# A state-space layer and its feed-forward block on one core: the first product of the later groups as seven block products, in a new order

## The chip, the core and the metric

The kernel runs on one core of a Trainium2 chip. The core has TensorE (PE; its weight loads are listed apart as PEld), VectorE (DVE), ScalarE (ACT), GpSimd (POOL) and SyncE (SP), which here issues the DMAs. Each engine works off its own queue. The metric is the time of one execution in device microseconds, lower is better. All arithmetic is fp32.

## The reference

The first part is a Mamba-2 scan over 4 batches, 8 heads, 768 positions, head size 32 and state size 16; the second is a feed-forward block over the 3072 tokens with 256 features:

```
y = ssd(x, a, B, C)              # intra-chunk products, plus state carried between chunks
x = y transposed to (3072, 256)
h = x @ w_in                     # 256 -> 2048
g = h * sigmoid(1.702 * h)
out = g @ w_out                  # 2048 -> 256
```

The weights and the scan inputs are drawn at random; `w_in` and `w_out` reach the kernel as 64-bit floats and are rounded to fp32 on VectorE and ScalarE in the first group.

## The kernel before

The tokens are cut into six groups g = 0 to 5 of 512. A group is made of four chunks of 128 tokens, and two chunks are a pair p, so that group g consists of pairs 2g and 2g + 1. Everything is transposed for the products: `yT[g]` holds the scan's result, features by tokens, in two 128-row halves.

The scan. `load(p)` (L102) fetches B, C and x of a pair, six DMAs; `spread` (L198) fetches a chunk's decays from a scratch tensor, repeated over 128 partitions. `decay` (L313) runs one VectorE scan of 1024 elements for each chunk, and `ends` (L359) multiplies B by its last column. `turn` (L422) transposes B and C on TensorE (tp), copies them on ScalarE and scales them on VectorE (CsT). `gain` and `keep` (L490, L503) form a pair's share of the state (A, S). `score` (L457) multiplies C and B (cb, 32-row tiles, into a PSUM area of four banks) and `weigh` (L473) multiplies the result by the decays in one VectorE instruction of 2048 elements a pair. `finish` (L522) adds the inter-chunk part (L536) and the intra-chunk part (L547) in two PSUM banks and copies them to `yT` on ScalarE.

The first product. `hidden(g, f)` (L563) multiplies one of 16 blocks of 128 columns of `w_in` by `yT[g]`: two matmuls of 512 columns into one PSUM bank, and a Silu on ScalarE into half of `gT[g, j]`, with j = f // 2. So `gT[g, j]` is 256 hidden features by 512 tokens.

The second product. For group 0 it is plain (`project_all`, L582). From group 1 on it goes by Strassen's method in Winograd's form: `gT[g, j]` and the 256 x 256 block of `w_out` are taken as 2 x 2 blocks, `mix_w` (L602) forms four sums of weight blocks once, and `mix_g` (L617) four sums of activation blocks on VectorE, three instructions for each j. `product(g, j)` (L625) issues seven matmuls of 256 columns, each adding to its own accumulator in the four-bank area over the eight j. At the end of a group, `combine` (L658) copies two accumulators out on ScalarE and does five additions on VectorE; `give` (L676) transposes the result back and stores it. The last group ends in `end` (L685), which takes the products of j = 5 to 7 one accumulator after another.

The order is written by hand. Steps H0 to H7 (two `hidden`) and P0 to P7 (one `product`) alternate, with the H steps three ahead (five in group 1), and the table `after[g]` hangs the rest on steps. `in_order` (L20) ties each engine's instructions to the order in which the program issues them. So an instruction that waits on TensorE, VectorE or ScalarE holds all that were issued after it on that engine.

The program takes eight banks of PSUM: four in the area (cb, ab, acc) and four (`bank`, L421) that are handed out in turn to everything else. The pools in SBUF that matter are `raw` (four buffers each for B, C, x), `gT` (eight buffers, shared by `gT`, the mixed blocks, u and c of `combine`), and the wide buffers of the weight rounding ("m", "p2").

Of the kernel before, what the change touches and what calls it, by code (L numbers as in the profile page):

```python
# [8 lines left out]
FP32 = mybir.dt.float32  # L9
U32 = mybir.dt.uint32  # L10
AF = mybir.ActivationFunctionType
ALU = mybir.AluOpType
# [22 lines left out]
def kernel(  # L35
# [27 lines left out]

    nc = tc.nc
# [27 lines left out]
    ps = ctx.enter_context(tc.tile_pool(name="ps", bufs=4, space=bass.MemoryType.PSUM))  # L92
    dram = ctx.enter_context(tc.tile_pool(name="dram", bufs=1, space=bass.MemoryType.DRAM))


    az = const.tile([P, NC, P], FP32, name="az")
    az0 = const.tile([P, CG, P], FP32, name="az0")
# [4 lines left out]
    def load(p):  # L102
        rb[p] = raw.tile([P, 2, NH, N], FP32, tag="b", name=f"b{p}", bufs=4)
        rc[p] = raw.tile([P, 2, NH, N], FP32, tag="c", name=f"c{p}", bufs=4)
        rx[p] = raw.tile([P, 2, NH, D], FP32, tag="x", name=f"x{p}", bufs=4)
        for dst, src in ((rb, B), (rc, C), (rx, x)):
            for k in range(2):
                b, c = divmod(2 * p + k, NC)
                sl = slice(c * P, (c + 1) * P)
                nc.sync.dma_start(out=dst[p][:, k], in_=src[b, :, sl, :].rearrange("h s d -> s h d"))  # L110
# [100 lines left out]
    def spread_rows(b):  # L211
        raf[b] = raw.tile([P, NC, P], FP32, tag="af", name=f"af{b}", bufs=2)
        nc.sync.dma_start(out=raf[b].rearrange("p c s -> p (c s)"),
                          in_=a[b].unsqueeze(1).to_broadcast([NH, N, S]))
# [22 lines left out]
    for p in range(PG, 2 * PG):  # L237
        load(p)
# [52 lines left out]
    same = const.tile([P, NH, D], FP32, name="same")  # L291
# [132 lines left out]
    def area(name):  # L424
        return ps.tile([P, R, 4 * P], FP32, tag="cb", name=name, bufs=1)

    def turn_only(p):
# [13 lines left out]
        if p < PG:  # L441

            s["tp"] = ssd.tile([P, 2, P], FP32, tag="CsT", name=f"C{p}", bufs=4)
            nc.scalar.activation(s["tp"], tp[:, 1], AF.Copy)

    def since_start(p):
# [5 lines left out]
        s["CsT"] = ssd.tile([P, 2, P], FP32, tag="CsT", name=f"CsT{p}", bufs=4)  # L452
# [69 lines left out]
    def finish(p, late=False):  # L522
        g, half = divmod(p, PG)
        b, c = divmod(2 * p, NC)
        s = st.pop(p)
        L = Ls.pop(p)
        if half == 0:
            yT[g] = ffn.tile([P, NK, TG], FP32, tag="yT", name=f"yT{g}")
        y = [bank(f"y{p}_{t}")[:, :2 * P].rearrange("p (k i) -> p k i", k=2)
             for t in range(NK)]  # L530

        def inter(k, start, stop):
            old = state[p][:, 0] if k else state[p - 1][:, 1]
            for t in range(NK):
                rows = slice(HB * N * t, HB * N * (t + 1))
                nc.tensor.matmul(  # L536
                    out=y[t][:, k], lhsT=old[rows], rhs=s["CsT"][rows, k],
# [3 lines left out]
        inter(0 if c else 1, True, False)  # L541
        if c and not late:
            inter(1, False, False)
        for k in range(2):
# [6 lines left out]
        if c and late:  # L551
            inter(1, False, True)
        state.pop(p - 1, None)
        for t in range(NK):
            nc.scalar.activation(  # L555
                yT[g][:, t, 2 * half * P:2 * (half + 1) * P],
                y[t].rearrange("p k i -> p (k i)"), AF.Copy)
# [4 lines left out]

    def hidden(g, f):  # L563
        j, i = divmod(f, 2)
        if i == 0:
            gT[g, j] = ffn.tile([P, 2, TG], FP32, tag="gT", name=f"gT{g}_{j}", bufs=NF // 2)
# [5 lines left out]
        nc.scalar.activation(gT[g, j][:, i], h, AF.Silu, scale=GELU_SCALE)  # L572

# [43 lines left out]
    def mix_g(g, j):  # L617

        B = gT[g, j].rearrange("p i (t e) -> p i t e", t=2)
        t = mixed_g[g, j] = ffn.tile([P, 4, HT], FP32, tag="gT", name=f"mg{g}_{j}", bufs=NF // 2)  # L620
        nc.vector.tensor_tensor(out=t[:, 0:2], in0=B[:, :, 1], in1=B[:, 0], op=ALU.subtract)  # L621
        nc.vector.tensor_tensor(out=t[:, 2], in0=B[:, 1, 1], in1=t[:, 0], op=ALU.subtract)  # L622
        nc.vector.tensor_tensor(out=t[:, 3], in0=B[:, 1, 0], in1=t[:, 2], op=ALU.subtract)  # L623

    def product(g, j, only=range(7)):  # L625
        if j == 0:
            a = area(f"acc{g}").rearrange("p r (t e) -> p (r t) e", t=2)
            acc[g] = [a[:, i] for i in range(7)], a
            if g == NG - 1:

                for i in range(4, 7, 2):
                    b = bank(f"acc{g}_{i}").rearrange("p (t e) -> p t e", t=2)
                    acc[g][0][i:i + 2] = [b[:, 0], b[:, 1]]
# [7 lines left out]
        for i in only:  # L641
            lhsT, rhs = terms[i]
            nc.tensor.matmul(out=acc[g][0][i], lhsT=lhsT, rhs=rhs,  # L643
                             start=(j == 0 and i % 2 == 0), stop=(j == NF // 2 - 1),
                             skip_group_check=True)

    def copies(g):
        u = ffn.tile([P, 4, HT], FP32, tag="gT", name=f"u{g}", bufs=NF // 2)
        c = ffn.tile([P, 2, 2, HT], FP32, tag="gT", name=f"c{g}", bufs=NF // 2)
        done[g] = u, c  # L650

        nc.scalar.activation(u[:, 0:4:3], acc[g][1][:, 0:4:3], AF.Copy)  # L652
        return u, c
# [31 lines left out]
    def end(g, j0):  # L685
# [27 lines left out]
        for i in (1, 0):  # L713
            cols = slice(i * P, (i + 1) * P)
            turn_out(g, 1, (i,), o[1 + i])
            ob = ffn.tile([P, 2, TG], FP32, tag="gT", name=f"ob{g}_1_{i}", bufs=NF // 2)
# [57 lines left out]
    narrow(1)  # L774

# [31 lines left out]
    at(in_project[0], 14, lambda: finish(PG + 1))  # L807
    for k in range(PG):
        at(in_project[0], 5 + 3 * k, lambda k=k: load(2 * PG + k))
# [3 lines left out]
    after = [{} for _ in range(NG)]  # L813
    for g in range(1, NG):
        n, places = (g + 1) * PG, after[g]
        chunks = range((g + 2) * CG, (g + 3) * CG) if g + 2 < NG else ()
        if g == 1:
            def late(p):
                gain(p)
                keep(p)  # L820
                score(p)
                weigh(p)

            at(places, "H0", lambda: decay(2 * CG), lambda: decay(2 * CG + 1), lambda: turn(n1))
            n1 = n
            at(places, "H1", lambda: late(n1), lambda: decay(2 * CG + 2),
               lambda: decay(2 * CG + 3), lambda: turn(n1 + 1))
            at(places, "H3", lambda: finish(n1), lambda: late(n1 + 1))
            at(places, "H4", lambda: finish(n1 + 1))
            for k, i in enumerate(("H4", "P0", "P2", "P4")):  # L830
                at(places, i, lambda k=k: mix_w(k))
            for j in range(NF // 2):
                at(places, f"P{j - 1}" if j else "H4", lambda j=j: mix_g(1, j))
        else:
            at(places, "H1", lambda g=g: mix_g(g, 0), lambda g=g: give(g - 1))
            if g + 1 < NG:
                at(places, "H0", lambda n=n: gain(n + 1), lambda n=n: keep(n + 1),
                   lambda n=n: score(n), lambda n=n: weigh(n))
                at(places, "H1", lambda n=n: score(n + 1), lambda n=n: weigh(n + 1))
            at(places, "H2", lambda g=g: mix_g(g, 1))  # L840
            for j in range(2, NF // 2):
                at(places, f"P{j - 2}", lambda g=g, j=j: mix_g(g, j))
            if g + 1 < NG:
                at(places, "H2", lambda n=n: finish(n))
                at(places, "P0", lambda n=n: finish(n + 1))
        for k, c in enumerate(chunks):
            at(places, f"P{k + 1}", lambda c=c: decay(c))
        if g + 2 < NG:
            for k in range(PG):
                p = (g + 2) * PG + k  # L850
                at(places, f"P{5 + k}", lambda p=p: turn(p))
                if k == 0:
                    at(places, "P5", lambda p=p: gain(p), lambda p=p: keep(p))
# [7 lines left out]
    for g in range(1, NG):  # L861
        if g + 2 < NG:
            for k in range(PG):
                load((g + 2) * PG + k)
            for b in range(NB):
                if (g + 2) * CG <= b * NC < (g + 3) * CG:
                    spread_rows(b)
                    at(after[g], "P4", lambda b=b: clip_rows(b), lambda b=b: decay_rows(b))
        ahead = 5 if g == 1 else 3
        steps = [f"H{j}" for j in range(ahead)]  # L870
        for j in range(NF // 2):
            steps += [f"P{j}"] + ([f"H{j + ahead}"] if j + ahead < NF // 2 else [])
        for step in steps:
            j = int(step[1:])
            if step[0] == "H":
                hidden(g, 2 * j)
                hidden(g, 2 * j + 1)
            elif g < NG - 1 or j < 5:
                product(g, j)
            for do in after[g].get(step, []):  # L880
                do()
            if g + 2 < NG and step in ("H1", "H3"):
                for k in range(2):
                    spread((g + 2) * CG + k + (2 if step == "H3" else 0))
        if g < NG - 1:
            combine(g)
# [33 lines left out]
```

## Time and profile before

| | us |
|---|---|
| median of three runs | 393.74 (393.49 to 393.83) |
| the profiled execution, its own time | 397.72 |
| its span | 396.0 |

The profile is of that one execution. Its parts count in different ways: busy time is what an engine spent in instructions, and weight loads (PEld) lie beside matmuls. The chain that ended last is followed back from the last instruction, at each step to what released it. Line numbers are those of the kernel before.

Busy time in stretches of the span, in us:

| stretch | TensorE | VectorE | ScalarE |
|---|---|---|---|
| 0 to 20 | 17.01 | 13.15 | 6.02 |
| 20 to 60 | 38.06 | 35.56 | 22.08 |
| 60 to 100 | 40.00 | 31.63 | 11.36 |
| 100 to 140 | 40.00 | 32.18 | 11.50 |
| 140 to 180 | 40.00 | 27.08 | 9.89 |
| 180 to 220 | 40.00 | 21.31 | 8.79 |
| 220 to 260 | 40.00 | 23.46 | 9.46 |
| 260 to 300 | 39.98 | 20.28 | 10.63 |
| 300 to 340 | 40.00 | 8.48 | 7.02 |
| 340 to 380 | 40.00 | 12.49 | 9.34 |
| 380 to 396 | 11.96 | 4.75 | 2.66 |

The largest groups on TensorE are the first product's entries (L569, 384 of them, 173.3 us) and the second's (L643, 560 in four groups by their operands). A matmul's recorded length overlaps that of the next one. The weight loads of the second product take 190 ns each.

### The profile page before, as it was taken

To read this page: it belongs to the slowest core of one execution; us is meant where nothing else is said; L and a number is where in the kernel's file an instruction comes from. 1 tells how busy PE (TensorE), PEld (TensorE's weight loads), DVE (VectorE), ACT (ScalarE), POOL (GpSimd) and SP (SyncE) were. 2 spreads that over 40 slices of the span, in tenths; PEclk is the share of its full clock that TensorE was granted. 3 is DMA by queue.
4 is the path that set the end of the run, shared out by engine and by line. 5 is a ranking of instruction groups with operands and counts; after the bars stand their busy time and mean duration, and the time that the engine had idled before them with its cause. 6 is when DMAs were issued, how large, how long until landed. Compare 5 with 4: busy or idle time off the path is not lost.

```text
span 396.0 us, 5009 instructions
## 1 busy us (share of the span) xinstructions
PE 387.0 (98%) x2024; PEld 246.9 (62%) x2024; DVE 230.4 (58%) x348; ACT 108.7 (27%) x201; POOL 10.2 (3%) x32
## 2 busy tenths in 40 slices
PE   7989999999999999999999999999999999999995
PEld 2543447787556778566668566667566567556674
DVE  3959999993879696754574753572661131423133
ACT  3226857210432112322112231213231211321210
POOL 5000000010000001000000000000000000000000
PEclk9599999999999999999999999999999999999999
DMA  8989566920988000097000080000010000010001
GB/s 144 241 240 155 188 213 151 171 106 8 150 262 119 21 1 2 0 276 96 2 0 0 2 263 3 0 0 2 2 55 2 0 0 0 2 53 0 0 2 53
DMA packets 85790, 29.52 MB, mean 75 GB/s; under 512 B 75720, under 2 KB 79240, under 8 KB 85768
## 3 DMA queue, kind: packets, MB, share of 16 engines
q1 hardware_dynamic: 85672, 29.07, 31.1%
q8 instruction: 16, 0.26, 0.3%
q10 hardware_dynamic: 96, 0.13, 0.1%
q14 instruction: 6, 0.05, 0.0%
HBM read 25.95 MB, written 3.24 MB: 74 GB/s over the span
## 4 chain that ended last, share of the span: by engine, by line
PE 95%; DVE 3%; issue 1%; POOL 0%
PE h L569 41%; PE acc L643 31%; PE o L588 7%; PE cb L468 3%; PE busy L345 3%; PE y L547 3%; PE y L536 2%; PE tp L432 1%; PE ab L327 1%; PE oT L673 1%; PE A L496 1%; PE rows L403 1%; DVE L L479 1%; DVE L L354 1%; DVE w_in L181 0%
## 5 line engine op out<-in xcount | busy, mean ns | idle before, releaser
L569 PE MATMUL h<-yT,w_in 128*128 128x512 f32 x384 | 173.3, 596 | 0.8 <-DVE w_in L181 0.8
L569 PEld LDWEIGHTS h<-yT,w_in 128*128 128x128 f32 x384 | 71.5, 190 | 79.5 <-issue 73.0
L572 ACT ACTIVATE gT<-h 128x512 f32<-128x512 f32 x96 | 57.2, 596 | 172.8 <-PE h L569 134.5
L621 DVE TENSOR_TENSOR mg<-gT 128x512 f32<-128x512 f32 x40 | 27.5, 688 | 94.8 <-ACT gT L572 91.7
L643 PE MATMUL acc<-mg,mw 128*128 128x256 f32 x240 | 58.0, 379 | 0.0
L643 PEld LDWEIGHTS acc<-mg,mw 128*128 128x128 f32 x240 | 45.6, 190 | 6.2
L643 PE MATMUL acc<-gT,w_out 128*128 128x256 f32 x160 | 41.7, 384 | 0.0
L319 DVE TENSOR_TENSOR_SCAN L<-a,idents 128x1024 f32<-128x1024 f32 x18 | 41.1, 2282 | 0.0
L643 PEld LDWEIGHTS acc<-gT,w_out 128*128 128x128 f32 x160 | 29.5, 190 | 15.0 <-issue 11.5
L479 DVE TENSOR_TENSOR L<-L,cb 128x2048 f32<-128x2048 f32 (+1 forms) x13 | 27.5, 2122 | 6.8 <-PE cb L468 6.4
L588 PE MATMUL o<-w_out,gT 128*128 128x256 f32 x128 | 29.3, 383 | 0.0
L588 PEld LDWEIGHTS o<-w_out,gT 128*128 128x128 f32 x128 | 23.8, 190 | 4.1 <-issue 0.7
L643 PE MATMUL acc<-gT,mw 128*128 128x256 f32 x80 | 23.5, 379 | 0.0
L643 PE MATMUL acc<-mg,w_out 128*128 128x256 f32 x80 | 23.5, 379 | 0.0
L555 ACT ACTIVATE yT<-y 128x256 f32<-128x256 f32 x24 | 7.9, 381 | 44.0 <-PE y L547 40.8
L623 DVE TENSOR_TENSOR mg<-gT,mg 128x256 f32<-128x256 f32 x40 | 17.0, 425 | 1.4
L622 DVE TENSOR_TENSOR mg<-gT,mg 128x256 f32<-128x256 f32 x40 | 17.0, 425 | 1.4
L354 DVE TENSOR_TENSOR_SCAN L<-ab,idents 128x512 f32<-128x512 f32 x12 | 13.8, 1204 | 5.9 <-PE ab L327 5.9
L643 PEld LDWEIGHTS acc<-mg,w_out 128*128 128x128 f32 x80 | 15.2, 190 | 2.1
L643 PEld LDWEIGHTS acc<-gT,mw 128*128 128x128 f32 x80 | 15.2, 190 | 2.1
L656 DVE TENSOR_TENSOR u<-acc,u 128x256 f32<-128x256 f32 (+1 forms) x10 | 5.3, 531 | 17.5 <-ACT u L652 14.3
L468 PE MATMUL cb<-CT,BT 32*128 32x256 f32 x192 | 14.9, 422 | 0.2
(86 smaller groups left out, 258.4 us busy)
## 6 DMA issues: line engine op xcount, KB each, us to landing
a<-scratch SPq DMA_DIRECT2D x18, 512.0 KB, 5.4
bits<-in_moe_w_out_dram SPq DMA_DIRECT2D x4, 1024.0 KB, 5.4
x<-in_x_dram SPq DMA_DIRECT2D x24, 128.0 KB, 4.1
out_dram<-ob SPq DMA_DIRECT2D x11, 256.0 KB, 2.2
bits<-in_moe_w_in_dram SPq DMA_DIRECT2D x4, 512.0 KB
bits<-in_moe_w_in_dram SPq DMA_DIRECT2D x2, 1024.0 KB
b<-in_B_dram SPq DMA_DIRECT2D x24, 64.0 KB, 3.3
c<-in_C_dram SPq DMA_DIRECT2D x24, 64.0 KB, 3.2
```

What stands on the lines that cost most here:

```text
L319: nc.vector.tensor_tensor_scan(out=Ls[p][:, k].rearrange("p r q i -> p (r q i)"), data0=ra[n], data1=idents.rearrange("p h i -> p (h i)"), ...
L345: nc.tensor.matmul(out=t, lhsT=ones, rhs=ones.unsqueeze(1).to_broadcast([P, 4, P]), start=True, stop=True, skip_group_check=True)
L354: nc.vector.tensor_tensor_scan(out=flat[p][:, r], data0=ab, data1=idents.rearrange("p h i -> p (h i)")[:, :2 * Q * P], initial=0.0, op0=AL ...
L468: nc.tensor.matmul(out=cb[:, r, k], lhsT=BT[rows, k], rhs=CT[rows, k].rearrange("p q i -> p (q i)"), start=True, stop=True, tile_position= ...
L479: nc.vector.tensor_tensor(out=Lv[:, k], in0=Lv[:, k], in1=cb.rearrange("p r k e -> p k r e")[:, k], op=ALU.mult)
L569: nc.tensor.matmul(out=h, lhsT=w_in[:, k, f * P:(f + 1) * P], rhs=yT[g][:, k], start=(k == 0), stop=(k == NK - 1))
L572: nc.scalar.activation(gT[g, j][:, i], h, AF.Silu, scale=GELU_SCALE)
L588: nc.tensor.matmul(out=o[k // 2][:, k % 2], lhsT=gT[g, f // 2][:, f % 2, k * P:(k + 1) * P], rhs=w_out[:, f], start=(f == 0 and k % 2 == 0 ...
L621: nc.vector.tensor_tensor(out=t[:, 0:2], in0=B[:, :, 1], in1=B[:, 0], op=ALU.subtract)
L622: nc.vector.tensor_tensor(out=t[:, 2], in0=B[:, 1, 1], in1=t[:, 0], op=ALU.subtract)
L623: nc.vector.tensor_tensor(out=t[:, 3], in0=B[:, 1, 0], in1=t[:, 2], op=ALU.subtract)
L643: nc.tensor.matmul(out=acc[g][0][i], lhsT=lhsT, rhs=rhs, start=(j == 0 and i % 2 == 0), stop=(j == NF // 2 - 1), skip_group_check=True)
```

## The change

From group 2 on, the first product goes by the same seven block products. For each j, `w_in`'s 256 columns and its 256 rows are 2 x 2 blocks A, and `yT[g]` is 2 x 2 blocks B of 128 features by 256 tokens. `mix_in` forms the sums of A once (in group 0), `mix_y` the sums of B once for a group, in three VectorE instructions like those of `mix_g`.

`first(g, j, i)` issues link i of chain j: one matmul of 256 columns. Links 1, 6, 7 and 4 add up in the same half of one PSUM bank X, and ScalarE copies the partial sum out after 1, 6 and 7; after 4 the bank is one quarter of h, and a Silu takes it from there. Links 5, 2 and 3 write the two halves of a second bank Y. The step "D" of a chain comes after 7, 5 and 2: one VectorE addition of 512 elements (Y and the copies of 1 and 7) gives two quarters of h, and a Silu in place follows. Link 3 adds to the half of Y that D has read, and is followed by a VectorE addition of 256 elements (with the copy of 6) and a Silu in place.

The order of groups 2 to 5 is written anew as strings: "2.6" is link 6 of chain 2, "P" the next single matmul of the second product, "M" `mix_g`, "C" `combine`. The last two of the eight `product` steps of a group now lie among the first two chains of the next group. `finish` is issued in three parts with links between them. The transposes, A and state work of the group after next stay at the end of a group. Group 1 keeps `hidden`, with its side work moved by some steps.

Buffers: `raw` has three of each kind instead of four, `gT` six, the mixed blocks three of their own (tag "mg", where `az` and two blocks of group 0 lie first); `same` and `az0` share buffers with BT and CT. Load 3 moves from the first loads to after the second rounded piece, and loads 4 to 9 move by some steps. In the last group the accumulators are four one-bank tiles in place of the area, and `copies` is two instructions there.

The diff, cut to its core:

```diff
-        rb[p] = raw.tile([P, 2, NH, N], FP32, tag="b", name=f"b{p}", bufs=4)
+        rb[p] = raw.tile([P, 2, NH, N], FP32, tag="b", name=f"b{p}", bufs=3)
...
-    for p in range(PG, 2 * PG):
-        load(p)
+    load(PG)
...
+    def mix_in(n):
+        t = wide.tile([P, PN], FP32, tag=("m", "p2")[n % 2], name=f"mi{n}").rearrange(
+            "p (j s e) -> p j s e", j=2, s=4)
...
+        for o, u, v, op in ((s1, a21, a22, ALU.add), (s2, s1, a11, ALU.subtract),
+                            (s3, a11, a21, ALU.subtract), (s4, a12, s2, ALU.subtract)):
+            nc.vector.tensor_tensor(out=o, in0=u, in1=v, op=op)
...
+    def first(g, j, i):
...
+        if i in "1674":
+            lhsT, rhs, copy = {"1": (A[:, 0, 0], B[:, 0, 0], s["ac"][:, 0]),
+                               "6": (S[:, 1], T[:, 2], s["b"]),
+                               "7": (S[:, 2], T[:, 1], s["ac"][:, 1]),
+                               "4": (A[:, 1, 1], T[:, 3], None)}[i]
+            nc.tensor.matmul(out=s["X"], lhsT=lhsT, rhs=rhs, start=i == "1", stop=i == "4",
+                             skip_group_check=True)
+            if copy is None:
+                silu(gT[g, j][:, 1, :HT], s["X"])
+            else:
+                nc.scalar.activation(copy, s["X"], AF.Copy)
+        elif i in "523":
+            lhsT, rhs, o = {"5": (S[:, 0], T[:, 0], s["Y"][:, 1]),
+                            "2": (A[:, 1, 0], B[:, 1, 0], s["Y"][:, 0]),
+                            "3": (S[:, 3], B[:, 1, 1], s["Y"][:, 1])}[i]
+            nc.tensor.matmul(out=o, lhsT=lhsT, rhs=rhs, start=s.pop("new", False), stop=i != "5",
+                             skip_group_check=True)
+            if i == "3":
+                c12 = gT[g, j][:, 0, HT:]
+                plus(c12, s["Y"][:, 1], s["b"])
+                silu(c12, c12)
+        else:
+            block(g, j)
+            c = gT[g, j].rearrange("p i (t e) -> p (i t) e", t=2)[:, 0:4:3]
+            plus(c, s["Y"], s["ac"])
+            silu(c, c)
...
+    for g in range(2, NG):
...
+        run(g, "0.1 P P 0.6 P P 0.7 P 0.5 P 0.2 P 0.D", seven(g - 1, 6))
+        run(g, "1.1 P 0.4 P P 1.6 P P 0.3 M P P C 1.7 1.5 1.2 1.D", seven(g - 1, 7),
+            M=lambda: mix_g(g, 0), C=lambda: combine(g - 1))
+        if more:
...
+            run(g, "2.1 1.4 2.6 2.5 2.7 2.2 1.3 s1 2.D w1 2.4 give 2.3 3.1 s2 w2 3.6 y1 3.7 y2 y3 3.5 "
+                "3.2 3.D", s1=lambda: score(n), w1=lambda: weigh(n), give=lambda: give(g - 1),
+                s2=lambda: score(n + 1), w2=lambda: weigh(n + 1), y1=a[0], y2=a[1], y3=a[2])
...
+            run(g, "P P 3.4 P P 3.3 P P P M", seven(g, 0), M=lambda: mix_g(g, 1))
+            run(g, "4.1 y1 4.6 4.5 y2 4.7 4.2 y3 4.D M", y1=b[0], y2=b[1], y3=b[2],
+                M=lambda: mix_g(g, 2))
...
+        else:
+            run(g, "2.1 1.4 2.6 2.5 2.7 2.2 1.3 2.D 3.1 2.4 3.5 3.6 2.3 3.2 3.7 3.D M",
+                M=lambda: mix_g(g, 1))
+        for j in range(5 if more else 4, NF // 2):
+            h = "{1}.1 P {0}.4 P {1}.6 P {0}.3 P {1}.7 P {1}.5 P {1}.2 P {1}.D M".format(j - 1, j)
+            run(g, h, seven(g, j - 4), M=lambda: mix_g(g, j - 2))
+            if most:
+                decay(chunks[j - 4])
...
+        run(g, f"P P {k}.4 P P {k}.3 P P P", seven(g, 4))
...
+        mix_y(g + 1)
+        run(g, "P P A P T P P P P B", seven(g, 5),
+            **{"A": lambda: most and advance(p), "T": lambda: most and turn(p + 1),
+               "B": lambda: most and advance(p + 1)})
+        mix_g(g, 7)
```

## The prediction

> **What bounds the kernel now.** I read first the busy shares, the row of granted clocks and the chain that ended last, on the page:
>
> ```profile
> PE 387.0 (98%) x2024; PEld 246.9 (62%) x2024; DVE 230.4 (58%) x348; ACT 108.7 (27%) x201; POOL 10.2 (3%) x32
> ...
> PEclk9599999999999999999999999999999999999999
> ...
> PE 95%; DVE 3%; issue 1%; POOL 0%
> ```
>
> TensorE is the bound: the chain is TensorE for 95%, and from 36 us to 391 us its pieces follow each other with no wait to speak of. A microsecond of matmul taken out is a microsecond won, a microsecond in which TensorE waits is one lost. Next, the chain in order of time (start, length, entries):
>
> ```profile
> 229.47 3.63 PE h L569 x8
> 233.10 0.65 PE y L536 x8
> 233.75 1.01 PE y L547 x32
> 234.76 3.22 PE acc L643 x14
> ...
> 243.04 3.02 PE acc L643 x14
> 246.06 3.43 PE h L569 x8
> ```
>
> Each fp32 matmul is two entries. Eight h entries take 3.43, so 0.429 us for 512 columns; fourteen acc entries take 3.02, so 0.216 for 256: a 256-column product is 0.432 (I call it a slot). After thin matmuls (y, cb, A) the first wide one costs 0.20 more (3.63 against 3.43, 3.22 against 3.02); after transposes it doesn't.
>
> Then the timeline where the second product of a group ends and is combined (TensorE's last acc entry ends at 219.02):
>
> ```profile
> 219.12 0.60 ACT L652 ACTIVATE u<-acc 128x512 f32<-128x512 f32 x1 [1.97 <-PE acc L643]
> 219.75 1.15 DVE L656 TENSOR_TENSOR u<-acc,u 128x256 f32<-128x256 f32 x2 [2.28 <-ACT u L652]
> ...
> 220.93 0.42 DVE L656 TENSOR_TENSOR c<-u 128x256 f32<-128x256 f32 x1
> 221.27 1.01 DVE L656 TENSOR_TENSOR c<-acc,u 128x512 f32<-128x512 f32 x2
> ```
>
> One copy of 0.60 and five additions in a row, 219.75 to 222.28, 2.53 in all; TensorE runs on with h meanwhile. Handing over costs 0.10 from TensorE's end to ScalarE, 0.03 from ScalarE to VectorE. An entry ends by the model 0.16 after its slot (0.379 less 0.216), so a reader starts 0.20 to 0.26 after the slot. Prices come from the groups:
>
> ```profile
> L572 ACT ACTIVATE gT<-h 128x512 f32<-128x512 f32 x96 | 57.2, 596 | 172.8 <-PE h L569 134.5 <-DVE Be L364 33.5 <-issue 4.5
> L555 ACT ACTIVATE yT<-y 128x256 f32<-128x256 f32 x24 | 7.9, 381 | 44.0 <-PE y L547 40.8 <-PE y L536 3.3
> L159 ACT ACTIVATE p<-p,edge 128x512 f32<-128x512 uint32 x4 | 2.9, 719 | 5.1 <-DVE p L148 5.1
> L277 ACT ACTIVATE X<-az,pick 128x256 f32<-128x256 f32 x6 | 2.6, 497 | 2.0 <-DVE az L269 2.0
> L656 DVE TENSOR_TENSOR u<-acc,u 128x512 f32<-128x512 f32 x4 | 2.8, 691 | 0.1
> L656 DVE TENSOR_TENSOR u<-acc,u 128x256 f32<-128x256 f32 x6 | 2.5, 424 | 17.4 <-ACT u L652 14.3 <-PE acc L643 3.0
> ```
>
> **Matmuls saved.** In groups 2 to 5 (counted from 0) 64 h entries become 112 of 256 columns: 64 x 0.429 - 112 x 0.216 = 27.46 - 24.19 = 3.27 a group, 13.1 in four. Their weight loads (190 ns) fit under 216, as acc's do.
>
> **Thin work cut in pieces.** `finish` is split around wide products, and A and cb no longer adjoin. I count four more exits from thin work in groups 2 and 3 and three in group 4: 11 x 0.20 = 2.2 lost.
>
> **The chains in the steady loop.** Link 6 needs the copy of link 1 out of the same bank, 7 that of 6, 4 that of 7. A copy is ready 0.26 + 0.38 + 0.05 = 0.69 after its slot; three slots (1.30) lie between 1 and 6 and between 6 and 7, more before 4. That hides it while ScalarE is free. ScalarE gains 32 x (three copies of 0.38, one silu of 0.38, one of 0.50 and one of 0.72, less two of 0.596) = 50 us, VectorE 32 x (0.42 + 0.69) = 36 us and mixing of 1.52 a group; both stay below a round of 14 slots (6.05 us): with a decay scan VectorE has 0.42 + 0.69 + 1.52 + 2.52 = 5.15. With the scan ahead of it the addition after link 3 comes late, link 7's copy behind it, and next link 6 some 0.1 late: 0.8 in eight rounds. Cost if that cover goes: 0.4 a round, 13 in all.
>
> **The start of each group: a new wait.** In the built order of groups 2 to 5 VectorE has, after chain 0's link 3: that link's addition, `mix_g(0)`, the five additions of `combine` for the group before, then chain 1's D addition. ScalarE has: silu of chain 0's last quarter, copy u, copy of 1.7, silu of chain 1's D, and only then the copy of 2.1, which link 2.6 needs on TensorE. From the end of 0.3's slot: addition 0.20 to 0.62; silu (0.50) to 1.15; `mix_g(0)` (1.52, VectorE 121.14 to 122.66 in the timeline) 1.18 to 2.70; combine (2.53) to 5.23; D addition (0.69) to 5.92; silu (0.70) to 6.65; copy (0.38) to 7.06; 2.6 at 7.1. TensorE has seven slots until then (P, P, 1.7, 1.5, 1.2, 2.1, 1.4): 3.02. So it stands for 4.1 us, with all its queue behind 2.6. Before, no matmul waited on combine: h's silu has no VectorE step ahead of it. The silus out of SBUF are not in the trace: between the PSUM rows (381, 596) and the SBUF rows (497, 719) the wait is 3.85 to 4.1; I take the SBUF rows. Four starts: 16.4.
>
> **Smaller waits after it.** In the same manner: 2.7 on the copy of 2.6 0.2, 3.6 behind VectorE's weighing 0.1, 5.6 0.1: 1.2 over groups 2 to 4. In group 5 no thin work and few P lie between: 2.7 0.2, 3.6 1.15 (copy of 3.1 behind the silu of D), 4.6 0.8, 5.6 0.3: 2.45. Before group 3, link 0.1 needs the bank of the transposes, which VectorE frees after a scan of rows (2.83): 0.9. With the loop's 0.8: 5.4, bounds 0 and 9.
>
> **The clock.** The only closing of the gate in this trace:
>
> ```profile
> 8.00:10.00 2.00, 0.63 (x4) 0.42 (x4) 2.00 (x2) 0.07 (x1) 0.00 (x0) 1.00 1.14 239
> 10.00:12.00 2.00, 1.62 (x2) 0.76 (x3) 2.00 (x3) 1.32 (x4) 0.00 (x0) 0.60 0.75 74
> ...
> 18.00:20.00 2.00, 2.00 (x3) 0.80 (x3) 1.96 (x6) 0.00 (x0) 0.00 (x0) 0.50 1.18 252
> 20.00:22.00 2.00, 2.00 (x5) 0.86 (x4) 0.22 (x2) 0.00 (x0) 0.00 (x0) 0.84 0.89 266
> ```
>
> The column after POOL is the granted clock. After idle times of 1.30 and 0.49 it falls to 0.5 at about 10.4, and comes back near 20.3, 3.5 us after wide matmuls began (16.77). A wait of 4.1 is longer than both, so I expect closings: 3.5 us at half clock lose 1.75, less some 0.25 that later waits absorb, 1.5. Where it falls against the gate isn't known: I take three starts of four, 4.5. Bounds: 0, and 14 if each closing lasts twice as long.
> The Trainium skill ("TensorE: Matmul & The Clock Gate", Part 1) has a free-running window of about 3.4 us, and the gate closes after an idle one. By that rule alone 4.1 us holds a whole idle window about one time in five, and the term would be some 1 us and the time near 406; but the row above closed on windows that were half busy.
>
> **What costs nothing.** `mix_in` (four times 1.5) fits VectorE's idle time from 90.8 to 97.1. Load 3, six DMAs of some 4 us, moves behind fetch 6 on SP's queue; it is needed some 30 us later, and its buffer is free from 27 us, so nothing stands behind it. Loads 5, 7 and 9 wait for buffers that have been read by then. Smaller pools (three raw, six gT, three mg) hold each buffer a round longer than its reader needs. If load 3 held SP's queue, w_out and group 1 would be late by microseconds.
>
> **Sum.** -13.1 + 2.2 + 16.4 + 5.4 + 4.5 = +15.4 on the profiled execution, 397.72 us (span 396.0): 413.1. The median of the runs shown is 393.74; the same amount gives 409.1.
>
> **Rivals.**
> Gate stays open through the waits: +10.9, 404.6. For it: waits of 0.28 to 0.48 at 26 to 32 us left the clock at 1.00. Against: 1.30 and 0.49 didn't.
> Worse: each closing lasts longer, or VectorE falls behind in the steady rounds and every chain waits 0.4 more: 8 to 13 more, 417 to 422. For it: 5.15 of 6.05 us leaves little. Against: only groups 2 and 3 have scans.
> Faster: VectorE reaches chain 1's D addition early, with mix and combine over, so that the wait at the group start is short. Then from link 1.2: 0.20 + 0.69 + 0.70 + 0.38 + handovers 0.1 = 2.1 against two slots, 0.86: wait 1.2 four times, and -13.1 + 2.2 + 5.4 + 4.9 = -0.6, 393.1; with all waits hidden -10.9, 382.8. It decides at 1.4 us a start: below that the change gains. I put it at 388. Against it: both queues hold combine ahead, and combine can't begin before the last P.
> Break-even, 394 to 400: the wait is 3.1, as if `mix_g(0)` hid, and the gate stays open. Little for it.
>
> **Chances.** Forecast 0.48 (406 to 413), open gate 0.28 (401 to 406), worse 0.13 (mostly over 418), break-even 0.04, faster 0.07. Leaving out some 0.2 at both ends: 400 to 418. Differences under 0.2% can't be told from no change here: faster 0.07, same 0.02, slower 0.91.
>
> **What would show it.** In the profile after: four waits of about 4 us of TensorE on ScalarE's copy (X before ac), one after each combine, with VectorE busy through them; the first product's entries at 216 ns outside them; digits below 9 in the clock row behind them. No such waits and a TensorE busy 97% would prove the main step wrong; waits without a fall of the clock would leave 404.6.

## The result and the profile after

The changed kernel takes 410.45 us (409.75 to 415.87, four runs); the kernel before, run beside it, 393.78 (393.49 to 395.87). The ratio of the means is 1.044, with a 95% interval of 1.035 to 1.054: slower by 16.7 us at the median, where 15.4 was forecast. The profiled execution took 409.75 us, with a span of 408.0.

The first lines of the page of the changed kernel, and its largest group of waits:

```profile
PE 380.8 (93%) x2216; PEld 282.3 (69%) x2216; DVE 272.5 (67%) x440; ACT 148.6 (36%) x330; POOL 10.4 (3%) x32
...
PEclk9999999999999999899999899999989999989999
...
PE 80%; DVE 13%; issue 3%; ACT 2%; DMA 1%; POOL 0%; ACTq 0%; POOLq 0%; DVEq 0%
...
L649 PE MATMUL X<-my,mi 128*128 128x256 f32 x128 | 41.9, 410 | 15.6 <-ACT ac L654 15.4
```

TensorE works 6.2 us less and still ends later. VectorE, 3% of the chain before, now holds 13% of it. Four digits of the clock row are 8, about a group apart. Of the waits of TensorE, 15.4 us lie ahead of links 6 (X from my and mi), on ScalarE's copy (L654); 14.3 of them are four waits of 3.57, one ahead of link 2.6 in each of groups 2 to 5.

The chain through the start of group 2 tells where (start, length, what):

```profile
157.64 0.45 PE Y L659 x2
158.11 0.44 DVE gT L759
...
159.02 0.70 DVE mg L618
...
159.75 0.44 DVE mg L619
...
160.21 0.42 DVE mg L620
160.63 0.35 DVE u L759
...
161.00 0.70 DVE u L759
...
162.07 1.01 DVE c L759 x2
163.08 0.61 DVE gT L759
...
164.25 0.37 ACT ac L654
...
164.67 0.70 PE X L649 x2
```

Link 0.3 (157.64) releases VectorE's addition; the first mixing (L618 to L620), the additions of `combine` (u, c) and the D addition of chain 1 (163.08) run in a row; then come a silu and the copy of link 2.1 on ScalarE, and only then link 2.6. TensorE had run out of work at 160.93. Link 2.1 had run in the slot from 160.07 to 160.50, so its copy could have begun by 160.8; it began at 164.25, because of the queue ahead of it.

The granted clock behind that wait is the column after POOL; where it stands at 0.5, the clock gate is called closed:

```profile
164.00:166.00 2.00, 1.33 (x5) 0.84 (x5) 0.00 (x0) 1.27 (x4) 0.00 (x0) 0.90 0.00 0
166.00:168.00 2.00, 2.00 (x5) 1.64 (x6) 0.00 (x0) 0.38 (x1) 0.00 (x0) 0.50 0.00 0
168.00:170.00 2.00, 2.00 (x19) 0.98 (x18) 1.02 (x2) 0.56 (x2) 0.00 (x0) 0.75 0.00 0
```

A mean of 0.90 over 2 us is 0.4 us at half clock, and a mean of 0.75 is 1.0 us: the gate is closed from 165.6 to 169.0, 3.4 us. The same happens at 230.4, 295.3 and 356.7, after each of the four starts.

The other waits of the changed kernel, from its timeline (start, length, and in brackets the idle time before and its releaser), are at link 5.1 (here in group 2), at link 0.1 ahead of group 3, at 2.6 as above, and at 3.6 and 4.6 in group 5:

```profile
185.93 0.70 PE L649 MATMUL X<-yT,w_in 128*128 128x256 f32 x2 [0.29 <-ACT yT L571]
...
213.72 0.70 PE L649 MATMUL X<-yT,w_in 128*128 128x256 f32 x2 [0.79 <-DVE CsT L457]
...
229.64 0.70 PE L649 MATMUL X<-my,mi 128*128 128x256 f32 x2 [3.57 <-ACT ac L654]
...
362.30 0.70 PE L649 MATMUL X<-my,mi 128*128 128x256 f32 x2 [0.74 <-ACT ac L654]
...
366.43 0.70 PE L649 MATMUL X<-my,mi 128*128 128x256 f32 x2 [0.41 <-ACT ac L654]
```

The bracket counts from the modelled end of the entry before, 0.16 after its slot, and the first product after a wait takes 0.53 to the next start instead of 0.43. So a wait costs its bracket and 0.26: 3.84 at each group start.

### The profile page after: what moved, and what is told of

Its sections match the earlier page's. It is cut to its first block, busy times and chain, and to the rows that moved or that the text cites. A ratio compares the mean times of both kernels' runs of the same rounds, so it can differ in the third digit from the quotient of the medians.

```text
span 408.0 us, 5632 instructions
## 1 busy us (share of the span) xinstructions
PE 380.8 (93%) x2216; PEld 282.3 (69%) x2216; DVE 272.5 (67%) x440; ACT 148.6 (36%) x330; POOL 10.4 (3%) x32
## 4 chain that ended last, share of the span: by engine, by line
PE 80%; DVE 13%; issue 3%; ACT 2%; DMA 1%; POOL 0%; ACTq 0%; POOLq 0%; DVEq 0%
PE acc L742 27%; PE X L649 13%; PE h L593 13%; PE Y L659 10%; PE o L685 7%; PE cb L472 3%; DVE L L483 3%; PE y L549 2%; DVE gT L759 2%; PE y L540 1%; PE tp L436 1%; PE ab L331 1%; DVE c L759 1%; DVE u L759 1%; DVE mg L618 1%
## 5 line engine op out<-in xcount | busy, mean ns | idle before, releaser
L627 ACT ACTIVATE gT<-gT 128x512 f32<-128x512 f32 x64 | 33.5, 524 | 97.9 <-DVE gT L759 97.9
L593 PE MATMUL h<-yT,w_in 128*128 128x512 f32 x128 | 57.4, 596 | 0.8 <-DVE w_in L186 0.8
L649 PE MATMUL X<-my,mi 128*128 128x256 f32 x128 | 41.9, 410 | 15.6 <-ACT ac L654 15.4
L759 DVE TENSOR_TENSOR gT<-Y,ac 128x512 f32<-128x512 f32 x32 | 22.0, 689 | 46.2 <-PE Y L659 45.4
L593 PEld LDWEIGHTS h<-yT,w_in 128*128 128x128 f32 x128 | 23.7, 190 | 29.3 <-issue 25.0
L649 PEld LDWEIGHTS X<-my,mi 128*128 128x128 f32 x128 | 23.1, 195 | 24.3 <-ACT ac L654 19.1
L654 ACT ACTIVATE ac<-X 128x256 f32<-128x256 f32 x64 | 24.1, 376 | 28.1 <-PE X L649 28.1
L596 ACT ACTIVATE gT<-h 128x512 f32<-128x512 f32 x32 | 19.0, 594 | 41.0 <-PE h L593 40.7
L618 DVE TENSOR_TENSOR mg<-gT 128x512 f32<-128x512 f32 x40 | 27.3, 683 | 1.9 <-ACT gT L627 1.9
L649 PE MATMUL X<-yT,w_in 128*128 128x256 f32 x64 | 19.7, 390 | 1.6 <-ACT yT L571 0.9
L659 PE MATMUL Y<-yT,mi 128*128 128x256 f32 x64 | 20.9, 411 | 0.0
```

The costliest lines, as they stand in the source:

```text
L593: nc.tensor.matmul(out=h, lhsT=w_in[:, k, f * P:(f + 1) * P], rhs=yT[g][:, k], start=(k == 0), stop=(k == NK - 1))
L627: nc.scalar.activation(o, i, AF.Silu, scale=GELU_SCALE)
L649: nc.tensor.matmul(out=s["X"], lhsT=lhsT, rhs=rhs, start=i == "1", stop=i == "4", skip_group_check=True)
L654: nc.scalar.activation(copy, s["X"], AF.Copy)
L659: nc.tensor.matmul(out=o, lhsT=lhsT, rhs=rhs, start=s.pop("new", False), stop=i != "5", skip_group_check=True)
L759: nc.vector.tensor_tensor(out=o, in0=v, in1=w, op=ALU.add)
```

## The experiments

The theory: the new order puts mixing, `combine` and the D addition ahead of one short copy, TensorE waits for it, and the wait also closes the clock gate. The first rival: the chains themselves (copies between links, more instructions on VectorE and ScalarE) are what costs. Ratios are of means, to runs of the kernel before on the same chip (median 395.7 in both sets, 393.3 to 397.9). Executions of one kernel fall into groups some 2 us apart, by how long the gate closes in the first 25 us, so differences of a few us are taken between the shortest executions, here 393.3 to 393.5 for before and 409.75 for after: 16.3.

**The queues' order, with TensorE's order as it is.**

```diff
-        run(g, "1.1 P 0.4 P P 1.6 P P 0.3 M P P C 1.7 1.5 1.2 1.D", seven(g - 1, 7),
+        run(g, "1.1 P 0.4 P P 1.6 P P 0.3 P P 1.7 1.5 1.2", seven(g - 1, 7))
...
-            run(g, "2.1 1.4 2.6 2.5 2.7 2.2 1.3 s1 2.D w1 2.4 give 2.3 3.1 s2 w2 3.6 y1 3.7 y2 y3 3.5 "
+            run(g, "2.1 1.D 1.4 2.6 C 2.5 2.7 2.2 1.3 s1 2.D w1 2.4 give 2.3 3.1 s2 w2 3.6 y1 3.7 y2 y3 M 3.5 "
```

> TensorE's order is that of the changed kernel; on VectorE and ScalarE the D addition of chain 1 goes ahead of combine, combine comes after the copy of 2.6, and mix_g(0) goes behind the second weighing. Theory (queue order behind combine makes the wait at 2.6): that wait falls from 3.6-3.8 us to about 0.3; 2.7 waits about 0.5 for its copy, and in groups 2 to 4 the first cb waits about 1.8 us for combine, since it needs the area. Sum per start about 2.5 instead of 4.0, and no closing of the clock gate: 396 to 399 us (402 to 405 if the gate still closes). Rival (what costs is ScalarE's and VectorE's extra work or the thin pieces, wherever combine stands): 408 to 411.

Measured 398.4 us (396.12 to 400.42), 1.0054 (1.002 to 1.0088). Its span was 394.4, and at the start of group 2:

```profile
160.42 0.59 PE L649 MATMUL X<-my,w_in 128*128 128x256 f32 x2
161.12 0.70 PE L649 MATMUL X<-my,mi 128*128 128x256 f32 x2
...
165.45 1.15 PE L472 MATMUL cb<-CT,BT 32*128 32x256 f32 x16 [1.59 <-DVE c L759]
```

Link 2.6 (161.12) comes 0.27 after the slot of 1.4 ends, where it came 3.74 after it. The scores wait 1.59 for the area that `combine` empties, once each in groups 2 to 4; group 5, which has no scores there, has two waits of 0.97 and 0.83 instead. The granted clock was 1.00 throughout. Between the shortest executions 13.6 of the 16.3 us are thus the place of `combine`, the first mixing and the D addition in two queues, with every matmul where it was (the same is done in the last group); what of it is the wait and what the clock, the next kernel tells. The chains themselves, which are all still there, don't cost that.

**TensorE kept busy through the wait.** Four matmuls of 512 columns of ones, into a bank that is overwritten next, go ahead of link 2.6:

```diff
-            run(g, "2.1 1.4 2.6 2.5 2.7 ...
+            run(g, "2.1 1.4 hold 2.6 2.5 2.7 ...
+    def hold(g, n):
+        t = bank(f"Y{g}_2")
+        for _ in range(n):
+            nc.tensor.matmul(out=t, lhsT=ones, rhs=ones.unsqueeze(1).to_broadcast([P, 4, P]),
+                             start=True, stop=True, skip_group_check=True)
```

> The changed kernel with four entry pairs of 512 columns (3.4 us of product of ones, into chain 2's Y bank before its first use, results overwritten) issued between links 1.4 and 2.6 in each of groups 2 to 5, so that TensorE works through the wait. Theory (each wait closes the gate for one window of 3.4 us, which costs 1.5 to 1.7 us): granted clock 1.00 through all four starts, 2.6 starts at the same distance from combine as before, time 403.5 to 405. Rival (after the wait ScalarE and VectorE pace the links, so the half clock costs nothing): clock 1.00 and 409 to 411.

Measured 405.21 us (403.95 to 408.16), 1.0238 (1.0186 to 1.0289): 0.2 above the range of the theory, and well under that of the rival.

```profile
162.73 0.59 PE L649 MATMUL X<-my,w_in 128*128 128x256 f32 x2
163.16 3.60 PE L985 MATMUL Y<-ones 128*128 128x512 f32 x8
166.90 0.70 PE L649 MATMUL X<-my,mi 128*128 128x256 f32 x2
```

The same 3.74 us pass between 1.4's slot (to 163.16) and 2.6, and nothing is won from the wait itself; but the gate stays open at the four starts. So, between the shortest executions, 5.8 of the 16.3 us are the gate, 1.45 a start.

**A new order.** Links 1 and 6 of chain 2 go ahead of the last products of the group before, the copies of `combine` (U) are split from its additions (C), which come after chain 2's D, and scores and `finish` after chain 3; the mixings move behind them.

```diff
-        run(g, "1.1 P 0.4 P P 1.6 P P 0.3 M P P C 1.7 1.5 1.2 1.D", seven(g - 1, 7),
+        run(g, "1.1 P 0.4 P 1.6 P 0.3 P 1.7 P 2.1 1.5 1.4 P 1.2 2.6 1.D P U 2.5 2.7 1.3 2.2 2.D 3.1 2.4 C "
+            "3.6 3.5 3.7 3.2 2.3 3.D", seven(g - 1, 7),
...
+            run(g, "s1 w1 3.4 give 3.3 4.1 s2 w2 4.6 y1 4.5 y2 4.7 y3 M 4.2",
...
+            run(g, "P P 4.4 P P y1 P y2 P y3 P 4.D M N", seven(g, 0), y1=b[0], y2=b[1], y3=b[2],
```

> New order around each group start: chain 2's links 1 and 6 come before the last products of the group before, combine goes behind chain 2's D addition, the scores and finish come after chain 3. Nothing is left out. Theory: no wait over 1 us at any group start, clock 1.00, first product's 13 us kept less 2 for thin pieces and 1 to 1.5 per start: 385 to 390 us, faster than both kernels. Rival (VectorE or ScalarE can't keep up in the stretch without second products, whatever the order): waits of 3 us or more come back elsewhere, 397 to 405.

Measured 392.18 us (391.74 to 396.16), 0.9937 (0.9901 to 0.9973): faster than both kernels, above the range expected. Its new start, on ScalarE and then on TensorE:

```profile
164.51 0.63 ACT L627 ACTIVATE gT<-gT 128x512 f32<-128x512 f32 x1 [0.35 <-DVE gT L762]
165.05 0.37 ACT L656 ACTIVATE ac<-X 128x256 f32<-128x256 f32 x1
...
165.47 0.70 PE L649 MATMUL X<-my,mi 128*128 128x256 f32 x2 [0.92 <-ACT ac L656]
```

The copy of 3.1 stands behind the silu of 2.D, and link 3.6 waits 0.92: the same fault, one chain later and smaller.

**`finish` in one piece**, in the changed kernel.

```diff
-            run(g, "2.1 1.4 ... 3.1 s2 w2 3.6 y1 3.7 y2 y3 3.5 "
+            run(g, "2.1 1.4 ... 3.1 s2 w2 3.6 y1 y2 y3 3.7 3.5 "
...
-            run(g, "4.1 y1 4.6 4.5 y2 4.7 4.2 y3 4.D M", ...
+            run(g, "4.1 y1 y2 y3 4.6 4.5 4.2 4.7 4.D M", ...
```

> The changed kernel with finish in one piece again (three thin-to-wide changes fewer in each of groups 2 to 4; 4.7 trades places with 4.2 to keep two slots behind 4.6). Theory (each change from thin to wide costs 0.2 us): 9 x 0.2 = 1.8 us less, 408.2 to 409.2. Rival (the pieces cover the copies of the links, and without them TensorE waits as long as it saves): 410 to 411.5.

Measured 410.33 us (409.51 to 415.1), 1.0378 (1.0326 to 1.043): no gain over 410.45, and the number that the rival gave. For the theory it is a miss, but it doesn't settle the price, since in its trace the gate was closed twice as long at the starts of groups 3 and 4 (from 227.8 and 292.6, 6.8 us each). Of these, 5.4 and 5.9 us lie behind the end of the wait, so that TensorE lost some 2.7 and 2.9 us there instead of 1.7 each. Without these 2.2 us the profiled execution of 410.09 would have come to 407.9, 1.9 under the changed kernel's; this is an estimate. The next pair asks again, where no wait closes the gate.

**The new order, mended, and then `finish` whole.** The first starts from the kernel of the new order: it moves the copy of 3.1 forward (and a scan of rows, which was meant to end the wait ahead of group 3). The second starts from the first, and adds whole finishes.

```diff
-        ... U 2.5 2.7 1.3 2.2 2.D 3.1 2.4 C "
+        ... U 2.5 2.7 1.3 3.1 2.2 2.4 2.D C "
```

```diff
-            run(g, "s1 w1 3.4 give 3.3 4.1 s2 w2 4.6 y1 4.5 y2 4.7 y3 M 4.2",
+            run(g, "s1 w1 3.4 give 3.3 4.1 s2 w2 4.6 y1 y2 y3 4.5 4.7 M 4.2",
...
-            run(g, "P P 4.4 P P y1 P y2 P y3 P 4.D M N", ...
+            run(g, "P P 4.4 P P y1 y2 y3 P P P 4.D M N", ...
```

> The order of c_order with two edits: link 1 of chain 3 goes ahead of link 2 of chain 2, so that its copy stands ahead of the silus of chain 2 on ScalarE; and the decays' rows of group 2 are worked out one step earlier. Theory (what c_order lost on its expectation is one wait of 0.92 us in each of the four groups, at link 6 of chain 3, because the copy of link 1 of chain 3 stands behind a silu that waits for VectorE, and 0.79 us once ahead of group 3, each with 0.27 more on the first pair after it): four times 1.2 and once 1.06 go, 5.9 in all, from 392.2 to 386 to 388. Rival (the silus of chain 2 are late whatever stands ahead of them, and the next link that needs ScalarE waits instead): 390 to 392.

> e_order2 with the three parts of each finish in one piece, which takes away 12 changes from thin to wide matmuls, here where no gap closes the clock gate. Theory (each such change costs 0.2 us, as the prediction priced it): 2.4 under e_order2. Rival (the change costs nothing of its own, or what it saves comes back as a wait for the copies that the parts had covered, as in d_whole): within 0.6 of e_order2.

The first measured 389.06 us (388.91 to 391.39), 0.9858 (0.9819 to 0.9897): 3.1 of the 5.9 expected. In its timeline:

```profile
164.13 0.70 PE L649 MATMUL X<-my,mi 128*128 128x256 f32 x2
164.67 0.59 PE L661 MATMUL Y<-my,mi 128*128 128x256 f32 x2
165.55 0.70 PE L649 MATMUL X<-my,mi 128*128 128x256 f32 x2 [0.28 <-ACT b L656]
...
208.82 0.70 PE L649 MATMUL X<-yT,w_in 128*128 128x256 f32 x2 [0.85 <-DVE CsT L457]
```

The wait of 0.92 is gone, and link 3.7 (165.55) waits 0.28 for the copy of 3.6 instead: half theory, half rival. The wait ahead of group 3 stayed (208.82, 0.85). That doesn't clear the scan of rows. In the changed kernel it stands right ahead of the VectorE instruction that frees the bank:

```profile
211.59 1.76 DVE L390 TENSOR_TENSOR_SCAN since<-af,first 128x768 f32<-128x768 f32 x1 [0.52 <-POOL af L383]
213.26 0.40 DVE L457 TENSOR_TENSOR CsT<-tp,since 128x256 f32<-128x256 f32 x1
```

In the mended order it begins at 204.79, but VectorE then works on without a gap (an addition, a mixing of blocks) to CsT at 208.34: from 199.66 on it idles only 0.52, ahead of the scan. So the scan, moved within one run of work, can still have made CsT late; no run takes it out of that run, and the cause is argued from the traces alone.

The second measured 386.15 us (385.85 to 390.14), 0.980 (0.9751 to 0.9848), the fastest kernel here. Against the first, 2.9 us for 12 changeovers is 0.24 each (3.1 us and 0.26 between the shortest executions); the waits at the group starts are the same in both. The first `finish` of group 2 in the kernel with parts, then in the one without:

```profile
172.32 0.49 PE L540 MATMUL y<-CsT,S 64*128 64x128 f32 x4
172.74 0.70 PE L661 MATMUL Y<-my,mi 128*128 128x256 f32 x2
173.37 0.64 PE L549 MATMUL y<-L,x 128*32 128x128 f32 x16
173.94 0.70 PE L649 MATMUL X<-my,mi 128*128 128x256 f32 x2
174.57 0.64 PE L549 MATMUL y<-L,x 128*32 128x128 f32 x16
175.15 0.70 PE L661 MATMUL Y<-yT,w_in 128*128 128x256 f32 x2
```

```profile
176.54 0.49 PE L540 MATMUL y<-CsT,S 64*128 64x128 f32 x4
176.96 1.08 PE L549 MATMUL y<-L,x 128*32 128x128 f32 x32
177.97 0.70 PE L661 MATMUL Y<-my,mi 128*128 128x256 f32 x2
178.50 0.59 PE L649 MATMUL X<-my,mi 128*128 128x256 f32 x2
```

Alone between thin pieces, a wide product takes 0.63 from its start to the next start (172.74 to 173.37); behind another wide one 0.43; and the two halves of the thin work take 0.57 each (173.37 to 173.94) against 1.01 in one piece (176.96 to 177.97).

**Doses of the wait.** What gap closes the gate? One kernel moves only the first mixing behind chain 1's D, which shortens the wait; the other has two matmuls of ones where the earlier kernel had four, which leaves its second half idle.

```diff
-        run(g, "1.1 P 0.4 P P 1.6 P P 0.3 M P P C 1.7 1.5 1.2 1.D", seven(g - 1, 7),
+        run(g, "1.1 P 0.4 P P 1.6 P P 0.3 P P C 1.7 1.5 1.2 1.D M", seven(g - 1, 7),
```

> The changed kernel with the first mixing of blocks (1.56 us of VectorE) moved from ahead of the combination's additions to behind them. The wait at link 6 of chain 2 should fall from 3.57 us to some 2.7, and with it 4 x 0.9 = 3.6 go from 410.45. Theory one (the clock gate closes when half of a 3.4 us window is idle: in the changed kernel's four closings 1.8 to 2.75 us of the window before were idle, and 1.6 us did not close it): it closes at two to four of the four starts, 403 to 407. Theory two (a whole idle window of 3.4 us is needed): it closes at none, 400.5 to 402.

> The changed kernel with two idle matmuls of 512 columns (0.86 us each, of ones, into a bank that is overwritten next) at the head of the wait, where b_hold had four: the wait's end is not moved, and some 1.9 us of it stay idle. Theory one (half of a window): the window is idle for 1 to 1.9 of 3.4 us, so the gate stays open at three or four of the four starts and the time is that of b_hold, 404 to 406.5. Rival (the gate looks at the length of a gap, with its bound between 1.6 and 1.9 us): it closes at all four, 409.5 to 411.

The first measured 404.78 us (404.04 to 406.7), 1.0249 (1.0209 to 1.029). The wait fell to 2.64 to 2.70, and in its trace the gate closed at groups 3 and 5 and stayed open at 2 and 4, and the time is in the range of theory one: a whole idle window isn't needed. (Half a window isn't an exact bound either; the last section has the idle times.) The second measured 408.23 (407.07 to 410.74), 1.0336 (1.0295 to 1.0378), between its two expectations: both miss. The clock in its trace behind the starts of groups 3 and 5:

```profile
228.00:230.00 2.00, 0.45 (x2) 0.43 (x3) 0.56 (x1) 1.18 (x3) 0.00 (x0) 1.00 0.00 0
230.00:232.00 2.00, 2.00 (x7) 1.35 (x6) 0.00 (x0) 0.40 (x2) 0.00 (x0) 0.60 0.00 0
...
354.00:356.00 2.00, 0.22 (x1) 0.00 (x0) 1.08 (x3) 0.88 (x3) 0.00 (x0) 1.00 0.00 0
356.00:358.00 2.00, 1.88 (x8) 1.35 (x8) 0.00 (x0) 0.69 (x4) 0.00 (x0) 1.00 0.00 0
```

The gate closed after the first and not after the second, with waits of 1.86 and 1.85 ahead of them. It closed at three starts of four.

## Why the prediction held, step by step

**The sum.** On the two profiled executions the difference is 409.75 - 397.72 = 12.0, less than forecast. But in the one before the gate was closed from 10.4 to 20.6 us, and in the one after it wasn't: group 1's first h starts at 97.95 before and at 93.70 after, 4.3 us earlier, about what parts the longest executions of the kernel before from the shortest (397.8 and 393.5). From there on the change costs 16.3, which agrees with the shortest executions. The sum was made against an execution with a loss of its own.

**Matmuls saved**, -13.1: a link takes its 0.432 in the steady rounds. In the mended order with whole finishes 7.6 us of it are seen (393.4 to 385.85); its trace has 3.8 us of waits left (four of 0.54, one of 1.10 and one of 0.58, reckoned as below), and 1.7 are not assigned. So 13.1 is shown as the price of the links, and not as a gain in time.

**Thin work in pieces**, +2.2: 0.24 to 0.26 a changeover instead of 0.20, so 2.6 to 2.9. The kernel that should have shown it in the changed order didn't; only the pair with the gate open did.

**The start of each group**, +16.4: measured 4 x 3.84 = 15.4. The queue was right in its order and in what ended last: link 2.6 came 6.76 us after 0.3's slot (157.91 to 164.67) where 7.1 was worked out. So TensorE stood for 3.74, just under the range given (3.85 to 4.1), and the slower first product adds 0.10. Two things differ, here in the timeline:

```profile
158.57 0.42 ACT L627 ACTIVATE gT<-gT 128x256 f32<-128x256 f32 x1 [1.37 <-DVE gT L759]
...
163.00 0.68 DVE L759 TENSOR_TENSOR gT<-Y,ac 128x512 f32<-128x512 f32 x1
...
163.72 0.63 ACT L627 ACTIVATE gT<-gT 128x512 f32<-128x512 f32 x1 [3.81 <-DVE gT L759]
164.25 0.37 ACT L654 ACTIVATE ac<-X 128x256 f32<-128x256 f32 x1
```

The silus out of SBUF, which I had priced by other instructions from SBUF at 0.50 and 0.70, took 0.42 and 0.63, 0.15 less together. And an instruction can begin before the recorded end of the one ahead of it on its engine, which the sum left out: the copy began 0.10 before the silu's end (164.25 and 164.35), the D addition 0.08 before the end of `combine` (163.00 and 163.08).

**Smaller waits**, +5.4: with 0.26 added to each bracket, 1.05 before group 3 (0.9 was forecast, and the scan of rows stands where it was said to), 1.00 and 0.67 in group 5 (1.15 and 0.8), and three of 0.55 at link 5.1, which I had not seen: it needs a bank that the copy of yT frees. Link 2.7 came 0.2 late in group 2 as forecast (165.64 to 165.84). The steady rounds, for which 0.8 was put down because of the scans, show no wait over 0.2. In all some 5, by another list than mine.

**The clock**, +4.5: closings at four starts, not three. A closing of 3.413 us at half clock holds 1.7 us of work back, and held open 1.45 a start came back: 5.8 to 6.8. This is the term that was most too small. The length of a closing, 3.5, was near, but its reading was not: the row's mean of 0.84 over 20 to 22 us puts the opening at 20.6 and not at 20.3, 3.9 us after the wide matmuls began, and that closing lasted 10.2 in all. What the lengths go by stands in the last section.

**What costs nothing**: nothing showed. From 93.7 us on no matmul waits over 0.2 us for a transfer, for a buffer of the smaller pools or for `mix_in`.

With the matmuls saved taken as forecast, the terms as measured give -13.1 + 2.8 + 15.4 + 5 + 5.8 to 6.8 = 15.9 to 16.9, against 16.3 between the traces. That the forecast of 15.4 came within 1 us of this is in part luck: the starts were 1.0 and the smaller waits 0.4 too dear, the clock 1.3 to 2.3 and the thin pieces some 0.6 too cheap.

The rivals. With the gate open the forecast was +10.9 (404.6); the kernel with four matmuls of ones shows 10.6 between the shortest executions (403.95). The faster case needed `combine` out of the way of chain 1's D, and the orders that do this give 386 to 398. Its bound of 1.4 us a start fits: the queue order, with waits of 1.59 and the gate open, is 2.7 slower than before. Break-even, 394 to 400, was tied to a wait of 3.1 with the gate open, but the prediction's own terms then give +6.9, 400.6. The kernel with the mixing moved comes near that wait (2.64 to 2.70 in brackets, 2.9 to 3.0 with the 0.26); there the gate closed at two starts, and it took 404.8. Of the worse case, VectorE kept up in the steady rounds. Longer closings may be what one of the four executions of the changed kernel had, 415.87 us at a mean clock of 0.962 against 0.983 in the profiled one; it has no trace.

## What to carry to other kernels

Before a chain of links that each need a copy is put into an order, write down for every copy what stands ahead of it on its own engine, and what that waits for; a copy of 0.38 us here cost 3.8 a group because a silu ahead of it waited for an addition that stood behind three mixing instructions and five other additions. A step that ends a stage (here `combine`) goes behind the additions and copies that the next stage's matmuls need, not ahead of them, unless what it frees is needed sooner: in the queue order the scores waited 1.59 for its area. Fewer matmul columns pay only if the order keeps TensorE fed: the same seven products gave 1.044 in one order and 0.980 in another.

## What the hardware showed beyond this

The gate's closings begin on a grid and last whole steps of it. In the changed kernel's clock record, which the trace keeps, each lasts 3.413 us, and they begin 64.85, 64.85 and 61.44 us apart, 19, 19 and 18 steps; with `finish` in one piece two of four last 6.827, two steps, where the wait went on for 1.47 and 0.96 us after the closing began. Laid over the waits of groups 2 to 5 (counted from the end of the slot, to some 0.02), the grid gives the idle time in the window that ends where the gate closed, or did not:

| kernel | idle us in a 3.413 us window, gate then closed | gate stayed open |
|---|---|---|
| changed | 2.49, 2.61, 1.80, 2.82 | 1.93 |
| mixing moved | 2.36, 2.60 | 1.58, 2.07 |
| `finish` in one piece | 1.74, 2.27, 2.78, 2.46 | 2.00 |
| two matmuls of ones | 2.02, 2.02, 1.81 | 2.01 |
| queue order | | 1.75, 1.76, 1.75 |

From 2.27 us on it always closed, up to 1.58 it never closed anew; from 1.74 to 2.07 it did either, and what decides there is open. One estimate, fitted to these traces and not tested by a run: if the windows end 0.25 us before the record shows the clock change, all 13 closings follow 1.99 us or more of idle time, and no window above 2.02 stays open, which would be a single bound near 2.0. The Trainium skill ("TensorE: Matmul & The Clock Gate", Part 1) gives a free-running window of 3413 ns, which these records show to the nanosecond. Its section "HAM oscillation — how this bites in real kernels" states the abstract rule as no idle gaps above about 3.4 us; the measurement here is stricter, since gaps of 2.0 us closed the gate.

The groups of executions 2 us apart (393.5, 395.7 and 397.8 for the kernel before) go with the first 25 us: there the ten traces show the gate closed for 0 (six), 6.8 (two) or 10.2 us (two). The mean clocks of the kernel before in the three groups, 1.00, 0.991 and 0.987, fit the same three lengths. The profiled execution of before, at 397.72, had 10.2.
